# Eight of the twelve transposed chunk pairs turned by the DMA crossbar instead of TensorE

## The chip, the cores and the metric

One core of one Trainium2 chip runs the whole program. The metric is device time in microseconds (us). A run counts as slow when it is over 1.5% above the fastest run of the same kernel.

## The reference, cut to what matters

Two stages. The first is a chunked state-space scan with 4 batches x 8 heads, 768 steps, head width 32 and state width 16. The second is a gated feed-forward over the 3072 x 256 result.

```python
CB = np.einsum('bhin,bhjn->bhij', Cc, Bc)            # C and B of a chunk
M = CB * L                                           # decays and causal mask
y_intra = np.einsum('bhij,bhjd->bhid', M, xc)
y_inter = np.einsum('bhin,bhnd->bhid', Cc, state) * decay_to_i[:, :, :, None]
# ... state update ...
gate = np.maximum(x @ w_gate, 0.0)
val = x @ w_val
return (gate * val @ w_out).astype(np.float32)
```

Both products with C contract over the state dimension, so the kernel needs B and C with the state on the partitions, while they arrive with the tokens on the partitions: each must be turned.

## The kernel before: what the change and the argument touch

The tokens are worked in 12 pairs of 128-token chunks. Pairs 0 to 2 use a wider layout and are not touched. For each later pair GpSimd scales B and C by their decays into a token-major bf16 tile, TensorE turns four 128x128 blocks into PSUM, and ScalarE or VectorE copies them out, C twice, with the heads of the other half zeroed.

```python
def scale_bc(p, eng):
    b, c0 = p // PPB, 2 * (p % PPB)
    s = st[p]
    bs = att.tile([128, 4, 128], BF16, tag="bs", name="bs")
    src = s["bcr"].rearrange("s i j (t q) n -> s (i j) t q n", t=2)
    f = scaleBC[:, b, c0:c0 + 2].rearrange("s c j h -> s (c j) h")
    for t in range(2):
        eng.tensor_tensor(out=bs.rearrange(...)[:, :, t], in0=src[:, :, t], in1=f[...], op=ALU.mult)
    ...
# turn(p):   four nc.tensor.transpose into the PSUM tile "tp"
# tevac(p):  BT <- tp[0] (ScalarE); CT[:, t] <- tp[1] * tmask[:, t] (VectorE, or ScalarE twice)
```

The feed-forward of one 512-token block b is the filler in which the next two pairs, P and Q, are prepared. In the timelines shown below each engine keeps to the program's order (GpSimd: scaling, cast, mask; SyncE: transposes and loads), and SyncE issues nearly all the DMAs from one queue.

```python
for b in range(1, NBLK):
    P, Q, W = 2 * b + 2, 2 * b + 3, 2 * b + 1
    for n in (P + 2, P + 3):
        if n < NPAIR:
            load(n)                                  # 6 DMAs each, on SyncE
    ...
    for f in range(n, NF):
        gv(b, f)                                     # gate and value matmuls
        if b == 1 and at("scale P", 99, 6):
            scale(P, nc.gpsimd, nc.gpsimd)
        if at("scale Q", 9, 6, 4):
            scale(Q, nc.gpsimd, nc.gpsimd)
        if at("scale next P", 11, 11, 9) and P + 2 < NPAIR:
            scale(P + 2, nc.gpsimd, nc.gpsimd)
        if at("turn P", 9, 6, 5):
            turn(P); tevac(P, nc.scalar, nc.vector)
        if at("turn Q", 99, 8, 8):
            turn(Q); tevac(Q, nc.scalar, nc.scalar)
    ...
    inter(P, 0)          # state product, reads CT
    fout(b, 0)
    G(P)                 # B and C product, reads BT and CT
    sums(P); gevac(P)    # gevac: GpSimd's causal mask on part of gs
    ...
    fout(b, 2)
    inter(P, 1)
    Dm(P)                # diagonal product, reads gs
    sums(Q); G(Q)        # (order cut; the details differ by block)
```

## Time and profile before

| what | value |
|---|---|
| time | 127.55 us, median of 3 (126.92 to 127.69) |
| span of the profiled run | 125.4 us |
| TensorE busy | 119.2 us (95%) |
| ScalarE, VectorE, GpSimd busy | 82.0, 88.3, 42.3 us |
| SyncE's DMA queue | 47.9% of 16 engines' span |

TensorE is busy nearly all the time, so a column of busy shares alone says little. The question is where TensorE is ever made to wait. The prediction below shows the lines for that. Two further lines are used later, from the chain of waits (start, length, what): the first half group of block 1 and the last output group. Between these two marks the two kernels differ only by the change.

```profile
32.55 1.99 PE gv L612 x16
...
121.22 1.35 PE o L633 x24
```

The stretch is 121.22 - 32.55 = 88.67 us. What lies ahead of it, the start with its weight loads, is the same code in both kernels apart from four tile clearings on GpSimd.

### The profile page before, as it was taken

What the parts mean: (1) busy time and instruction counts of PE and PEld (TensorE: products, weight loads), DVE (VectorE), ACT (ScalarE), POOL (GpSimd) and SP (SyncE); (2) the same over time, 40 slices, a digit from 0 to 9 for tenths busy, and PEclk for the clock granted to TensorE, in tenths of its full rate; (3) what the DMA queues carried; (4) which work ended last, traced back from release to release, by engine and by line L of the source; (5) the groups of instructions that cost most, each with busy time, mean ns of one, the idle gap of its engine ahead of it and who ended that gap; (6) DMA issues with size and microseconds to landing.
All of it is one profiled execution on the core that took longest, in us unless ns stands there. A gap on an engine that the chain in (4) does not pass through costs nothing.

```text
span 125.4 us, 3648 instructions
## 1 busy us (share of the span) xinstructions
PE 119.2 (95%) x1400; PEld 83.2 (66%) x1400; DVE 88.3 (70%) x196; ACT 82.0 (65%) x185; POOL 42.3 (34%) x86
## 2 busy tenths in 40 slices
PE   6879799899999999999999999999999999999990
PEld 6656585378686578874477865577864577854790
DVE  4795888754799675998673899664989655687510
ACT  0568588835788843787945787935887745876410
POOL 6599863127445016800511801421700033000000
PEclk9999999999999999999999999999999999999999
DMA  3999999987898999196950399920400002200022
GB/s 66 215 172 204 172 216 197 144 106 90 95 105 222 113 116 98 44 200 75 120 70 0 104 167 112 98 40 0 156 16 0 0 0 89 84 0 0 0 89 84
DMA packets 72305, 12.15 MB, mean 97 GB/s; under 512 B 65904, under 2 KB 72288, under 8 KB 72288
## 3 DMA queue, kind: packets, MB, share of 16 engines
q1 hardware_dynamic: 66048, 8.84, 47.9%
q0 software_dynamic: 3184, 2.36, 12.6%
q10 hardware_dynamic: 3056, 0.72, 2.7%
q8 instruction: 11, 0.18, 0.6%
q14 instruction: 6, 0.05, 0.1%
HBM read 11.13 MB, written 3.15 MB: 114 GB/s over the span
## 4 chain that ended last, share of the span: by engine, by line
PE 83%; DMA 9%; ACT 2%; DVE 1%; issue 1%; POOL 1%; DVEq 0%; POOLq 0%
PE o L639 25%; PE gv L612 16%; PE val L597 13%; PE gate L594 13%; DMA wo<-in_moe_w_out_dram 9%; PE w L180 2%; PE y L569 2%; PE g L481 2%; PE tp L321 2%; PE y L558 1%; ACT gs L389 1%; PE o L633 1%; PE g L372 1%; POOL gs L385 1%; PE A_ps L528 1%
## 5 line engine op out<-in xcount | busy, mean ns | idle before, releaser
L601 DVE TENSOR_TENSOR h<-r,val 128x512 bf16<-128x512 bf16 x44 | 29.5, 686 | 8.8 <-ACT r L600 7.2
L639 PE MATMUL o<-wo,h 128*128 128x256 bf16 x276 | 32.8, 273 | 0.5 <-DMA wo<-in_moe_w_out_dram 0.5
L600 ACT ACTIVATE r<-gate 128x512 bf16<-128x512 f32 x44 | 25.9, 600 | 6.0 <-PE gate L594 4.0
L639 PEld LDWEIGHTS <-h 128*128 128x128 bf16 x276 | 25.9, 98 | 5.6 <-issue 1.5
L597 PE MATMUL val<-yT,wv 128*128 128x512 bf16 x88 | 26.2, 379 | 0.0
L594 PE MATMUL gate<-yT,wg 128*128 128x512 bf16 x88 | 26.2, 379 | 0.0
L618 DVE TENSOR_TENSOR h<-r,gv 128x256 bf16<-128x256 bf16 x56 | 22.5, 418 | 2.7 <-ACT r L615 1.8
L615 ACT ACTIVATE r<-gv 128x256 bf16<-128x256 f32 x56 | 21.4, 385 | 2.5 <-PE gv L612 0.4
L612 PE MATMUL gv<-yT,wv 128*128 128x256 bf16 x112 | 21.4, 273 | 0.7 <-DMA wv<-in_moe_w_val_dram 0.7
L612 PE MATMUL gv<-yT,wg 128*128 128x256 bf16 x112 | 21.4, 273 | 0.1
L506 DVE TENSOR_TENSOR gs<-g,maskUT 128x512 bf16<-128x512 f32 x18 | 11.6, 686 | 11.7 <-issue 9.6
L489 POOL TENSOR_SCALAR_AFFINE_SELECT gs<-gs 128x512 bf16<-128x512 bf16 (+1 forms) x18 | 9.0, 523 | 31.3 <-ACT gs L500 31.3
L291 POOL TENSOR_TENSOR bs<-bcr,scaleBC 128x256 bf16<-128x256 f32 x18 | 11.0, 633 | 21.3 <-PE gate L594 6.3
L597 PEld LDWEIGHTS <-wv 128*128 128x128 bf16 x88 | 8.6, 98 | 10.4
L594 PEld LDWEIGHTS <-wg 128*128 128x128 bf16 x88 | 8.2, 98 | 7.0
L612 PEld LDWEIGHTS <-wv 128*128 128x128 bf16 x112 | 10.9, 98 | 2.2 <-DMA wv<-in_moe_w_val_dram 0.9
L612 PEld LDWEIGHTS <-wg 128*128 128x128 bf16 x112 | 10.2, 98 | 2.0 <-issue 0.2
L500 ACT CAST gs<-g 128x512 bf16<-128x512 f32 x9 | 5.3, 589 | 6.7 <-PE g L481 6.7
L582 ACT CAST yT<-y 128x512 bf16<-128x512 f32 x9 | 5.3, 586 | 5.3 <-PE y L569 2.7
L180 PE MATMUL w<-warm 128*128 128x128 bf16 x49 | 5.0, 265 | 1.1 <-DVE tmask L154 1.1
L540 DVE TENSOR_TENSOR Sm<-A_ps,smask 128x256 bf16<-128x256 f32 x15 | 5.7, 415 | 0.0
L180 PEld LDWEIGHTS <-warm 128*128 128x128 bf16 x58 | 4.6, 118 | 1.7 <-DVE tmask L154 1.0
(108 smaller groups left out, 120.6 us busy)
## 6 DMA issues: line engine op xcount, KB each, us to landing
xr<-in_x_dram SPq DMA_DIRECT2D x19, 128.0 KB, 3.8
out_dram<-ob SPq DMA_DIRECT2D x3, 512.0 KB, 3.1
bcr<-in_C_dram SPq DMA_DIRECT2D x19, 64.0 KB, 3.5
bcr<-in_B_dram SPq DMA_DIRECT2D x19, 64.0 KB, 3.7
out_dram<-ob SPq DMA_DIRECT2D x4, 256.0 KB, 2.4
wo<-in_moe_w_out_dram POOLq DMA_DIRECT2D x1, 768.0 KB, 11.0
xr<-in_x_dram SPq DMA_DIRECT2D x2, 256.0 KB, 8.1
wg<-in_moe_w_gate_dram POOLq DMA_DIRECT2D x1, 384.0 KB, 6.2
```

The costliest lines, as they stand in the source:

```text
L180: nc.tensor.matmul(out=w, lhsT=warm, rhs=rhs, start=True, stop=True)
L291: eng.tensor_tensor(out=bs.rearrange("s k (q t n) -> s k t q n", q=4, t=2)[:, :, t], in0=src[:, :, t], in1=f[:, :, 4 * t:4 * t + 4].to_bro ...
L489: nc.gpsimd.affine_select(out=dst, in_=dst, pattern=[[0, n], [1, 128]], compare_op=ALU.is_ge, fill=0.0, base=0, channel_multiplier=-1)
L506: nc.vector.tensor_tensor(out=d[:, q], in0=g[q], in1=m, op=ALU.mult)
L594: nc.tensor.matmul(out=g, lhsT=wg[:, k, fs], rhs=yT[:, k, tk], start=(k == 0), stop=(k == 1))
L597: nc.tensor.matmul(out=v, lhsT=wv[:, k, fs], rhs=yT[:, k, tk], start=(k == 0), stop=(k == 1))
L600: nc.scalar.activation(r, g, AF.Relu)
L601: nc.vector.tensor_tensor(out=fst[b][:, f], in0=r, in1=v, op=ALU.mult)
L612: nc.tensor.matmul(out=gv_[:, j], lhsT=w[:, k, fs], rhs=yT[:, k, tk], start=(k == 0), stop=(k == 1), skip_group_check=True)
L615: nc.scalar.activation(r, gv_[:, 0], AF.Relu)
L618: nc.vector.tensor_tensor(out=fst[b][:, f, u * 256:(u + 1) * 256], in0=r, in1=gv_[:, 1], op=ALU.mult)
L639: nc.tensor.matmul(out=o[:, ts % 2], lhsT=fst[b][:, f, ts * 128:(ts + 1) * 128], rhs=wo[:, f], start=(f == 0), stop=(f == NF - 1), skip_gr ...
```

## The change

The intent is to take 32 transposes off TensorE and the copies behind them off ScalarE and VectorE. The token-major tile is widened to six blocks (B of two chunks, C with the first half of the heads, C with the second half, zeros elsewhere), so that one DMA with transpose (through the crossbar of the title) gives BT and both halves of CT in SBUF. Four such tiles are cleared once; later scalings overwrite only the non-zero parts. In block 1 the loads of pairs 6 and 7 are moved behind the transposes of pairs 4 and 5 respectively.

```diff
+    FIRST = 4
+    NTOK = 4
+    tok = [glob.tile([128, 6, 128], BF16, name="tok%d" % i) for i in range(NTOK)]
     def scale_bc(p, eng):
+        if p >= FIRST:
+            bs = tok[p % NTOK]
+            ...
+            for t in range(2):
+                for j in range(2):
+                    eng.tensor_tensor(
+                        out=dst[:, t, j * (1 + t)], in0=src[:, j, :, t],
+                        in1=f[:, j, :, 4 * t:4 * t + 4].to_broadcast([128, 2, 4, N]),
+                        op=ALU.mult)
+            turned = att.tile([128, 6, 128], BF16, tag="turned", name="turned", bufs=4)
+            nc.sync.dma_start_transpose(out=turned, in_=bs.rearrange("s k c -> s (k c)"))
+            s["B"] = [bs[:, i] for i in range(2)]
+            s["BT"] = turned[:, 0:2]
+            s["CT"] = turned[:, 2:6].rearrange("s (t i) m -> s t i m", t=2)
+            return
@@ before fout(0, 0)
+    for t in tok:
+        nc.gpsimd.memset(t, 0.0)
@@ block loop
-            if n < NPAIR:
+            if n < NPAIR and b > 1:
                 load(n)
@@
             if b == 1 and at("scale P", 99, 6):
                 scale(P, nc.gpsimd, nc.gpsimd)
+                load(P + 2)
             if at("scale Q", 9, 6, 4):
                 scale(Q, nc.gpsimd, nc.gpsimd)
+                if b == 1:
+                    load(P + 3)
@@
-            if at("turn P", 9, 6, 5):
-                turn(P)
-                tevac(P, nc.scalar, nc.vector)
-            if at("turn Q", 99, 8, 8):
-                turn(Q)
-                tevac(Q, nc.scalar, nc.scalar)
```

## The prediction

> **What bounds the kernel now.** I read the engines' busy shares first, then the waits of TensorE, then the chain of waits in order of time, and last the timelines of SyncE and GpSimd around the first turned pairs.
>
> ```profile
> PE 119.2 (95%) x1400; PEld 83.2 (66%) x1400; DVE 88.3 (70%) x196; ACT 82.0 (65%) x185; POOL 42.3 (34%) x86
> ...
> 33.00:122.60 89.60, 89.56 (x943) 62.17 (x941) 64.92 (x131) 61.88 (x136) 22.90 (x42) 1.00 0.48 76
> ```
>
> The first line is the page's busy time; the second is a stretch of the table by windows, from 33.0 to 122.6 us. Over these 89.60 us TensorE is busy 89.56 us at full granted clock, and the list of TensorE's waits for 36 to 118 us is empty. So in the part that the change touches the end is set by the plain sum of TensorE's work: what leaves this stream shortens the kernel one for one, if nothing that it then waits for comes later than now.
>
> ```profile
> 39.17 0.43 PE val L597 x2
> 39.60 0.22 PE tp L321 x4
> 39.83 0.43 PE gate L594 x2
> ...
> 41.55 0.22 PE tp L321 x4
> 41.78 0.43 PE gate L594 x2
> ...
> 48.91 0.28 PE L558 MATMUL y<-CT,Sm 128*128 128x128 bf16 x2
> 49.12 0.41 PE L569 MATMUL y<-gs,xb 128*32 128x128 bf16 x16
> ```
>
> The first lines are the chain (start, length): four transposes of a pair lie between two groups of matmuls and take 0.23 us until the next group starts. The last two are TensorE's timeline at pair 4's diagonal product, which needs the masked tile gs. It starts in the chain at 49.19 us, and no wait is listed.
>
> ```profile
> 46.42 1.20 POOL L291 TENSOR_TENSOR bs<-bcr,scaleBC 128x256 bf16<-128x256 f32 x2 [5.92 <-PE A_ps L528]
> 47.56 0.61 POOL L307 CAST xb<-xr 128x512 bf16<-128x512 f32 x1
> 48.13 1.00 POOL L489 TENSOR_SCALAR_AFFINE_SELECT gs<-gs 128x512 bf16<-128x512 bf16 x2
> ```
>
> This is GpSimd's timeline: scaling pair 6, casting its x, and only then the causal mask of pair 4, finished at 49.13 us, just before TensorE uses it at 49.19. There is no slack here at all: whatever delays pair 6's scaling or cast delays TensorE at pair 4.
>
> ```profile
> 35.82 1.80 SPq L117 DMA_DIRECT2D xr<-in_x_dram  x1
> 37.72 1.04 SPq L679 DMA_DIRECT2D out_dram<-ob  x2
> 38.85 0.44 SPq L116 DMA_DIRECT2D bcr<-in_B_dram  x1
> ...
> 41.63 0.92 SPq L116 DMA_DIRECT2D bcr<-in_C_dram  x1
> 42.59 0.58 SPq L117 DMA_DIRECT2D xr<-in_x_dram  x1
> ...
> 46.87 0.85 SPq L117 DMA_DIRECT2D xr<-in_x_dram  x1
> 51.98 0.38 SPq L657 DMA_DIRECT2D out_dram<-ob  x1
> ```
>
> SyncE's queue issues the loads of pairs 6 and 7 from 38.85 to 47.7 us, with the DMA engines full (share 0.94 to 1.21 from 38 to 48 us, 0.83 to 50, then 0.03 to 52). That is the second thing to watch: the stage has idle DMA time only after 50 us.
>
> **What the Trainium skill says.** "DMA: Bandwidth & Descriptors", section "DMA Transpose (X-bar)": a transpose by DMA must be issued from SyncE or ScalarE, write SBUF and have 2-byte elements; the change does so. The same page, "Latency and other measured facts", gives 261 GB/s as its effective rate with a non-contiguous middle dimension; "Advanced Engine Details and Errata", "X-Bar Transpose (TRN2)", expects 350 to 400 GB/s. No transpose by DMA is in the trace before, so it neither agrees nor disagrees. Third, "Issuing engines are not separate DMA queues" (first page) says that all queues share the same 16 engines; the trace agrees in that loads issued from 38.85 us on take a median 3.6 to 3.7 us to land while the engines are full. Fourth, "TensorE: Matmul & The Clock Gate", "Wait — 56ns, not 53.3ns?", has back-to-back matmuls of N = 128 start 55.6 ns apart; the chain shows 0.22 to 0.23 us for four transposes, 55 to 57 ns each: it agrees, and the 219 ns duration of each is latency.
>
> **The change part by part.**
> Removed from TensorE: 8 pairs x 4 transposes. The chain's eight pieces, each to the start of the next, are 0.23, 0.23, 0.23, 0.22, 0.22, 0.23, 0.22, 0.23 us: 1.81 us, all on the path. That is 1.4% of 127.55 us, and all that can be won.
> Removed from ScalarE: 8 copies of BT at 0.372 us and 8 masked copies of CT (two for each odd pair) at 0.478: 6.8 us. From VectorE: 4 masked copies of CT at 0.685: 2.7 us. Neither engine sets the pace in this stretch (62 and 65 of 90 us busy), so none of the 9.5 us shows in the time.
> Added to GpSimd: four half-size scalings for two, since C's halves go to separate blocks. The two of 128x256 take 1.20 us; pairs of 128x128 in the start took 0.78 to 0.79 us, so four take about 1.57: +0.37 us a pair. For pairs 4 and 5 that is hidden; for pair 6 it lies ahead of pair 4's mask. Four clearings of a 128x768 tile: 128 columns took 0.20 us and 256 took 0.31, so 768 take about 0.75 and four 3.0 us. They fall into GpSimd's 3.85 us of idling from 23.67 to 27.52 us, so cost nothing, with 0.8 us to spare.
> Added to the DMA: eight transposes of 128x768 bf16, 196.6 KB each. At the page's 261 GB/s one occupies the engines 0.75 us (estimate); the rows are cut at 256 bytes and there is the end of each transfer, so I take 1.2 us, with 0.75 to 3 possible.
> Moved: pair 6's loads go behind pair 4's transpose, pair 7's behind pair 5's. Pair 4's tile is scaled at 34.05 + 1.57 = 35.6 us, but SyncE is busy issuing until 38.8; so the transpose goes out at 38.85, behind the 512 KB of output that hold the engines until about 40.2 us. It lands at about 42, and its first reader, the state product, now starts at 44.37 - 0.45 = 43.9: met. Pair 6's loads slip by the same 1.2 us. C was issued at 41.63 and takes a median 3.6 us: 45.2 becomes 46.4; x at 42.59 plus 3.8: 46.4 becomes 47.6. GpSimd: scaling 46.4 to 48.0, cast to 48.6, first mask of pair 4 (0.64 us) to 49.25, second to 49.65. TensorE, now 0.45 us early, arrives at 48.74 and waits 0.5 to 0.9 us. (The old scaling waited for a bs buffer until 46.42; the new tile is free, so that wait falls away and the load takes its place.)
> Pair 5's transpose lands near 48 us; G of pair 5 comes at 49.1 plus the stall: met. Pair 6's goes out after pair 7's loads, about 51 us, and is needed after 62. Pair 7's stands behind pair 9's loads, whose issue ends at 63.0 and whose data end near 64.5; with 1.2 us of its own and the slip still left from earlier it lands about 66 to 67.5, against G of pair 7 at 67.86 - 0.9 + 0.7 = 67.7: just met. Pair 9's lands near 84 against 85.5. Pairs 8, 10 and 11 have 10 us or more.
> Sum: -1.81 + 0.7 for the mask of pair 4 + 0.4 as the expected value for pairs 7 and 9 being now and then late = -0.7 us, 126.9 us.
>
> **The rivals.**
> (a) All transposes hidden: -1.8 us, 125.7 us. For it: pair 6's loads may land well before the medians that I used, since GpSimd in the trace waited for the buffer, not for data, and its cast found x ready. Against it: the mask of pair 4 ended only 0.06 us before its use.
> (b) The transposes hold the DMA engines longer, 2 us each. Then pair 6's loads cost 1.5 us of stall at pair 4, and pair 7's transpose lands at about 69.8 us against 68.5, another 1.3: -1.8 + 2.8 = +1.0, 128.6 us. For it: the engines are full from 38 to 48 us, so every microsecond of transposing moves the loads; the loads themselves are short packets and the skill's rates are for large transfers. At 3 us each this becomes -1.8 + 2.5 + 3 = +3.7, 131 us, and the verdict slower.
> (c) The relief of ScalarE and VectorE gives more than TensorE's 1.8 us. Against it: TensorE has no listed wait in this stretch, so there is nothing to give back. I give it little.
>
> **Range and chances.** From 125.7 (a) to a little above (b), 129.6; the middle is 126.9. Faster by over 2% means below 125.0 us, under the floor of what is removed: 3%, for a gain that I can't see. Slower by over 2% means above 130.1 us, for which a transpose must cost about 2.6 us of engine time or block the queue in a way that I don't foresee: 15%. Within 2%: 82%.
>
> **What would show it.** The chain of the new kernel should have no tp pieces after 31 us, and TensorE should have one or two waits: at the diagonal product of pair 4 on GpSimd's mask (0.5 to 0.9 us near 49 us), and perhaps at G or the state product of an odd pair on the transposing DMA. The landing time of the transposes tells (a) from (b): 2 to 4 us if I am right. GpSimd's scaling of pairs 4 to 11 should show 32 instructions of 128x128 in place of 16 of 128x256, about 1.6 us a pair. I am wrong if TensorE waits for a transpose of pair 4 near 44 us, if the waits sum to over 1.8 us, if the clearings push GpSimd past 27.5 us and delay pair 2's mask, or if the whole gain appears with no wait at all.

## The result, and the profile after

The changed kernel took 125.79 us (median of 4, 125.61 to 126.31) against 127.41 for the kernel before. Ratios in this document are the mean time of one kernel's fast runs over that of the other's of the same rounds, so not quite the ratio of the medians quoted (four_twice is an exception, see there). Here it is 0.9883, 95% interval 0.984 to 0.9927: some 1.5 us, within 2%. All results are correct.

The page's busy line and the long stretch from the table by windows (each engine's busy us, then clock, DMA share, GB/s):

```profile
PE 118.5 (96%) x1368; PEld 82.4 (66%) x1368; DVE 87.3 (70%) x192; ACT 76.8 (62%) x169; POOL 47.2 (38%) x106
...
33.00:120.80 87.80, 87.80 (x911) 60.49 (x910) 63.94 (x127) 56.95 (x120) 25.21 (x58) 1.00 0.57 95
```

TensorE still fills the stretch completely, at full clock, with 32 instructions fewer. ScalarE is 5 us lighter, VectorE 1 us, GpSimd 5 us heavier. The chain at the place where pair 4 was turned, at pair 4's diagonal product, and at the two marks of the stretch:

```profile
32.94 1.99 PE gv L636 x16
...
39.56 0.43 PE val L621 x2
40.00 0.43 PE gate L618 x2
...
49.13 0.34 PE y L593 x16
...
119.83 1.35 PE o L657 x24
```

The tp pieces are gone: a gate group follows the value group at once. The stretch is 119.83 - 32.94 = 86.89 us, 1.78 us shorter than before. The start was 0.39 us longer in this trace.

The turned tile, by its instructions (durations min/median/max in ns), and SyncE's queue line of the page:

```profile
L306 SPq DMA_TRANSPOSE turned<-tok x8: 1219/1231/1363, 38.7 to 88.8; - x8
...
DMA to landing us min/median/max: 2.7/3.2/3.4
```

```profile
q1 hardware_dynamic: 72448, 10.42, 54.7%
```

An issue holds the queue for 1.2 to 1.4 us and the data land 2.7 to 3.4 us after it. The queue took 54.7% of 124.0 us where it was 47.9% of 125.4: 67.8 - 60.1 = 7.8 us, or 0.97 us of packet time on all 16 engines for each transpose. Packet times can overlap (the kernel before has shares up to 1.21), so this is not a time for which the engines were shut to other transfers.

GpSimd and SyncE around pair 4 (timelines; the bracket is the idle time before, and what ended it):

```profile
45.67 1.63 POOL L301 TENSOR_TENSOR tok<-bcr,scaleBC 128x128 bf16<-128x128 f32 x4 [4.92 <-DMA bcr<-in_B_dram]
47.25 0.61 POOL L331 CAST xb<-xr 128x512 bf16<-128x512 f32 x1
47.81 0.99 POOL L513 TENSOR_SCALAR_AFFINE_SELECT gs<-gs 128x512 bf16<-128x512 bf16 x2
```

```profile
38.67 1.36 SPq L306 DMA_TRANSPOSE turned<-tok  x1
40.09 0.57 SPq L116 DMA_DIRECT2D bcr<-in_B_dram  x1
...
42.89 0.58 SPq L116 DMA_DIRECT2D bcr<-in_C_dram  x1
```

The wait for a free bs buffer (5.92 us, ended by the sums of pair 4) has become a wait for pair 6's load, as foreseen. It ended at 45.67 us, so the mask was done at 48.80 and TensorE came at 49.1: 0.3 us to spare, and no wait.

### The profile page after: what moved, and what is told of

It is laid out like the page before. It is cut to its first block, busy times and chain, and to the rows that moved or that the text cites. A ratio compares the mean times of both kernels' runs of the same rounds, so it can differ in the third digit from the quotient of the medians.

```text
span 124.0 us, 3586 instructions
## 1 busy us (share of the span) xinstructions
PE 118.5 (96%) x1368; PEld 82.4 (66%) x1368; DVE 87.3 (70%) x192; ACT 76.8 (62%) x169; POOL 47.2 (38%) x106
## 3 DMA queue, kind: packets, MB, share of 16 engines
q1 hardware_dynamic: 72448, 10.42, 54.7%
## 4 chain that ended last, share of the span: by engine, by line
PE 84%; DMA 7%; POOL 6%; DVE 1%; issue 0%; DVEq 0%; POOLq 0%
PE o L663 25%; PE gv L636 16%; PE val L621 15%; PE gate L618 15%; DMA wv<-in_moe_w_val_dram 7%; PE y L593 2%; PE g L505 2%; PE w L180 2%; POOL wg L189 2%; PE y L582 2%; POOL bs L277 1%; POOL wv L189 1%; PE o L657 1%; PE A_ps L552 1%; POOL xb L328 1%
## 5 line engine op out<-in xcount | busy, mean ns | idle before, releaser
L625 DVE TENSOR_TENSOR h<-r,val 128x512 bf16<-128x512 bf16 x44 | 30.2, 687 | 9.0 <-ACT r L624 7.9
L301 POOL TENSOR_TENSOR tok<-bcr,scaleBC 128x128 bf16<-128x128 f32 x32 | 12.0, 402 | 19.7 <-DMA bcr<-in_B_dram 18.7
L180 PE MATMUL w<-warm 128*128 128x128 bf16 x49 | 6.0, 300 | 1.1 <-DVE tmask L154 1.1
L180 PEld LDWEIGHTS <-warm 128*128 128x128 bf16 x58 | 5.4, 133 | 1.8 <-DVE tmask L154 1.1
```

Source lines behind the costliest of these rows:

```text
L180: nc.tensor.matmul(out=w, lhsT=warm, rhs=rhs, start=True, stop=True)
L301: eng.tensor_tensor(out=dst[:, t, j * (1 + t)], in0=src[:, j, :, t], in1=f[:, j, :, 4 * t:4 * t + 4].to_broadcast([128, 2, 4, N]), op=ALU. ...
L625: nc.vector.tensor_tensor(out=fst[b][:, f], in0=r, in1=v, op=ALU.mult)
```

## The experiments

All outputs are right.

### Is the gain TensorE's stream, and does it repeat?

Four kernels on one chip, five rounds each.

**after_again**: the changed kernel, unedited.

> The changed kernel once more, for a narrower interval. Theory (all eight transposes are hidden, TensorE's stream is 1.8 us shorter): ratio to before 0.986, some 125.7 us, and no wait of TensorE after 33 us. Rival (part of the gain is given back by a wait of about 0.3 to 0.7 us that the first trace did not catch): ratio 0.989 to 0.992.

**pe_turns_kept**: the work on TensorE comes back, result unused.

```diff
+            if at("turn P", 9, 6, 5):
+                spare_turn(P)     # four transposes of a constant tile into "tp"
+            if at("turn Q", 99, 8, 8):
+                spare_turn(Q)
```

> The changed kernel, and TensorE turns a constant tile at the old eight places, result unused (no copies, correct output). Theory (the gain is TensorE's stream alone): 1.8 us come back, ratio to before 0.999 to 1.001, 127.4 us. Rival (the relief of ScalarE and VectorE, 9.5 us of work, carries part of the gain): only part comes back, ratio 0.991 to 0.995.

**copies_kept**: the old copies come back on ScalarE and VectorE, from a constant tile.

```diff
+            if at("turn P", 9, 6, 5):
+                spare_copies(nc.scalar, nc.vector)
+            if at("turn Q", 99, 8, 8):
+                spare_copies(nc.scalar, nc.scalar)
```

> The changed kernel, and ScalarE and VectorE make the old copies of BT and CT at the old eight places from a constant tile, results unused. Theory: nothing changes against the changed kernel, ratio to before 0.986 to 0.988. Rival (relief of the two engines): 0.4 us or more is lost, ratio 0.990 or higher.

**from_pair_6**: pairs 4 and 5 as before, loads of 6 and 7 at their old place.

```diff
-    FIRST = 4
+    FIRST = 6
+            # turn(P)/tevac(P) and turn(Q)/tevac(Q) for pairs under FIRST; load(6), load(7) at the block's top
```

> Pairs 4 and 5 turned by TensorE as before, with the loads of 6 and 7 at their old place; pairs 6 to 11 by the crossbar. Theory: the gain goes by count, 6/8 of 1.8 = 1.35 us, ratio 0.9894, 126.0 us. Rival (the stage of pairs 4 and 5, where the DMA engines are full, costs what it saves): as much as the whole change, 0.986.

| kernel | median us | ratio to before | 95% interval | stretch us | against 88.67 |
|---|---|---|---|---|---|
| after_again | 126.39 | 0.9905 | 0.987 to 0.994 | 87.10 | -1.57 |
| pe_turns_kept | 127.28 | 0.999 | 0.9956 to 1.0023 | 88.68 | +0.01 |
| copies_kept | 126.32 | 0.9906 | 0.9875 to 0.9938 | 86.96 | -1.71 |
| from_pair_6 | 126.57 | 0.9935 | 0.9899 to 0.9971 | 87.70 | -0.97 |

The two marks in the chain of pe_turns_kept:

```profile
32.60 1.99 PE gv L636 x16
...
121.28 1.35 PE o L657 x24
```

With the transposes back on TensorE the stretch is as long as before to 0.01 us, though ScalarE and VectorE stay relieved. With the copies back on those two the ratio equals that of the changed kernel in the same call (0.9906 and 0.9905). Its absolute value lies outside the 0.986 to 0.988 that I had written down, because the changed kernel itself came out slower. So the gain is TensorE's stream alone, and the relief of the two other engines is worth nothing that these runs resolve.

The rule by count gave 1.35 us for six pairs; 0.97 was measured in the trace, 0.8 by the ratio. TensorE has a listed wait there: 0.24 us for VectorE's state tile at the state product of one later pair (88.18 us). The changed kernel's traces, with a TensorE stream that is shorter still, do not have it, so why it came up here is not shown. How the rest is made up was not traced.

The ratio of after_again lies in the rival's range, 0.989 to 0.992. In its trace 0.2 us of the 1.78 was missing, with no wait listed. The traces show the place: from the state product to G of pair 5, TensorE took 0.60 us in the first trace (48.86 to 49.46) and 0.80 in this one (49.08 to 49.88), with the mask done only at 49.55. That is the weak spot that the prediction named.

### Where is the slack, and what sets it?

Four kernels on one chip, three rounds each.

**loads_first**: the change without its reordering.

```diff
-            if n < NPAIR and b > 1:
+            if n < NPAIR:
                 load(n)
-                load(P + 2)       # behind scale(P)
-                if b == 1: load(P + 3)
```

> Changed kernel, but the loads of pairs 6 and 7 are issued at the block's top as before, ahead of the transposes of pairs 4 and 5. Theory (the queue is served in order, and 9 us of loads stand in it): pair 4's transpose is issued at about 47.7 us and lands 3.2 us later, 50.9, against its first use near 44.1: one wait of 6 to 7 us at the state product of pair 4, ratio to before about 1.04. Rival (order doesn't matter, a transpose of 0.8 to 1.2 us finds its way): ratio 0.99.

**four_twice**: pair 4's tile is turned twice.

```diff
+            if p == FIRST:
+                spare = att.tile([128, 6, 128], BF16, tag="spare", name="spare", bufs=1)
+                nc.sync.dma_start_transpose(out=spare, in_=bs.rearrange("s k c -> s (k c)"))
             nc.sync.dma_start_transpose(out=turned, in_=bs.rearrange("s k c -> s (k c)"))
```

> Changed kernel with pair 4's tile turned twice (first into a spare tile). Everything behind it in the queue, pair 6's loads first, slips by 1.25 us. Theory (pair 6's loads hold GpSimd, which stands between TensorE and pair 4's mask, with 0.3 us to spare at most): TensorE waits 0.7 to 1.2 us near 49 us at pair 4's diagonal product, +0.9 us against the changed kernel, ratio to before about 0.996. Rival (the loads have over 1 us of slack): no wait, ratio 0.989.

**four_twice_mask_first**: the same, with GpSimd's work on pair 6 moved behind pair 4's mask.

```diff
-            if at("scale next P", 11, 11, 9) and P + 2 < NPAIR:
+            if b > 1 and at("scale next P", 11, 11, 9) and P + 2 < NPAIR:
                 scale(P + 2, nc.gpsimd, nc.gpsimd)
@@ behind gevac(P) and states(P) of block 1
+                scale(P + 2, nc.gpsimd, nc.gpsimd)
```

> As four_twice, but GpSimd scales and casts pair 6 after pair 4's mask. Theory: the wait at pair 4's diagonal product is gone though the loads slip as much, ratio 0.988 to 0.990. Rival (the wait is one of the DMA or of the transposes of pairs 5 and 7 themselves): it stays, ratio 0.995 or more.

**twice**: every tile turned twice.

```diff
+            for _ in range(1):
+                spare = att.tile([128, 6, 128], BF16, tag="spare", name="spare", bufs=4)
+                nc.sync.dma_start_transpose(out=spare, in_=bs.rearrange("s k c -> s (k c)"))
             nc.sync.dma_start_transpose(out=turned, in_=bs.rearrange("s k c -> s (k c)"))
```

> Changed kernel with every tile turned twice. Theory: +0.9 us at pair 4's mask, up to 0.6 at pair 5's G, 1 to 2 at pair 7's G (its transpose lands at 66.3 against 67.4 in the changed kernel, and slips by 2.5): 2 to 3.5 us in all, 128 to 129.5 us, ratio 1.005 to 1.018. Rival (the DMA has room; only pair 4's stage is tight): +0.9 us, ratio 0.996.

| kernel | median us | ratio to before | 95% interval |
|---|---|---|---|
| loads_first | 135.66 | 1.0595 | 1.0509 to 1.0681 |
| four_twice | 128.97 (126.67 to 132.05) | 1.0082 (see below) | 1.0003 to 1.0161 |
| four_twice_mask_first | 129.29 | 1.0095 | 1.0011 to 1.0179 |
| twice | 131.53 | 1.0283 | 1.0205 to 1.0361 |

**loads_first.** TensorE's timeline has one wait, and the page's row of the granted clock shows what came after it:

```profile
51.09 0.40 PE L582 MATMUL y<-turned,Sm 128*128 128x128 bf16 x2 [7.12 <-DMA turned<-tok]
...
PEclk9999999999999955599999999999999999999999
```

The wait is 7.1 us where 6 to 7 were expected: the transpose was issued at 47.73 us behind the loads and landed at 51.04. The reordering of the loads is therefore worth more than the whole gain. The ratio was underestimated, 1.04 against 1.06. The clock row shows what the expectation had left out: for three slices of 3.3 us TensorE ran at about half its clock, part of it while waiting and part of it afterwards.

**twice.** The theory put the loss against the changed kernel at 2 to 3.5 us, a ratio of 1.005 to 1.018. The ratio is 1.0283: 3.6 us over the kernel before and, with the changed kernel's ratios of 0.9883 to 0.9933, 4.5 to 5.1 over the changed kernel. The trace is that of the fastest run (129.88 us, the others 131.47 to 131.74). TensorE's waits, and the table by windows for the time around them (TensorE's busy us stands second, the clock third from the end):

```profile
49.70 0.65 PE L596 MATMUL y<-gs,xb 128*32 128x128 bf16 x16 [0.80 <-POOL gs L516]
...
51.67 0.40 PE L508 MATMUL g<-turned 32*128 32x256 bf16 x8 [1.26 <-DMA turned<-tok]
```

```profile
48.00:50.00 2.00, 1.20 (x19) 0.92 (x17) 0.27 (x1) 0.10 (x1) 2.00 (x5) 1.00 1.31 76
50.00:52.00 2.00, 0.71 (x24) 0.35 (x23) 0.00 (x0) 0.59 (x1) 0.01 (x1) 1.00 1.06 111
52.00:54.00 2.00, 2.00 (x17) 1.57 (x14) 1.78 (x4) 0.86 (x2) 1.00 (x2) 0.69 1.17 108
54.00:56.00 2.00, 2.00 (x13) 1.39 (x10) 0.60 (x2) 1.19 (x3) 0.98 (x3) 0.50 1.35 155
```

The waits stand at the expected places: 0.8 us at pair 4's mask (0.9 expected), 1.3 at G of pair 5 (up to 0.6) and 0.2 at G of pair 7 (1 to 2). After them the clock falls to half. From the clock column of these windows and the next (0.95) that costs 2 x (0.31 + 0.50 + 0.05) = 1.7 us, so it lasts some 3.4 us (estimates). The stretch was 91.25 us, 4.36 longer than in the first changed trace: about 2.3 us of listed waits and 1.7 of clock; the rest, some 0.4 us, was not traced.

**four_twice and four_twice_mask_first.** The first one's profile fell in a run that counts as slow (132.05 us). That trace shows TensorE 3.1 us at pair 4's mask, but I take no size from it. The expected +0.9 us against the changed kernel cannot be judged from its fast runs either: there are two, 126.67 and 128.25. They average 127.46 us against 127.58 for the kernel before, 0.999, so the recorded 1.0082 can't be theirs alone, and I don't use it. The second was meant to remove the wait by moving GpSimd's work, and by that test the theory failed. The mask no longer held TensorE, but another wait stood next to it:

```profile
51.67 0.40 PE L508 MATMUL g<-turned 32*128 32x256 bf16 x8 [1.68 <-DMA turned<-tok]
...
70.21 0.40 PE L508 MATMUL g<-turned 32*128 32x256 bf16 x8 [0.64 <-DMA turned<-tok]
```

Pair 5's transpose landed 5.1 us after its issue (46.55 to 51.63), not 3.2. With 3.2 us it would have landed at 49.75, before TensorE came at 49.99 (51.67 - 1.68). So this wait comes from the late landing and not from the slip of the queue alone. In twice it is the same: 46.84 + 3.2 = 50.04, and TensorE came at 50.41. Pair 7's transpose took its usual 3.2 us but was issued late, at 66.93 us instead of 63.08. The stretch was 89.35 us, 2.46 longer than in the first changed trace, with 2.3 us of it in these two waits. The rival was half right: what held TensorE was transposes, but how much the slip alone would cost is not shown.

One thing stands beside both late landings. The rate of all transfers in twice, from 38 to 54 us in slices of 0.4 us:

```profile
GB/s 107 234 346 330 335 224 209 139 148 212 132 40 97 88 102 109 149 155 116 98 93 148 169 220 211 117 232 22 1 9 35 201 139 108 71 115 164 142 90 29
```

From 48.8 to 50.4 us it falls to 22, 1, 9 and 35 GB/s, while transposes stand unfinished. The trace's list of DMA packets has one of 16 KB, of the queue that the page calls instruction (q8), from 48.64 to 49.60 us; in four_twice_mask_first it runs from 48.40 to 49.65, with 1 to 10 GB/s from 49.2 to 50.4. In the three traces of the changed kernel this packet starts at 48.67 to 48.90, after pair 5's transpose has landed (47.82 to 48.70). That it holds the transposes up is likely but was not tested.

### With both edges moved

Four kernels on one chip, five rounds each. **before_again** is the kernel before against itself and **after_third** the changed kernel, both unedited.

> The kernel before against itself, as a check of the scatter and for a second trace of its start. Ratio 1.000 plus or minus 0.003. If the start up to the first half group of block 1 is again at 32.5 us, and the changed kernel's again at 32.9 or later, the start costs the changed kernel 0.4 us; if it moves by as much here, it is scatter of the weights' arrival.

> The changed kernel a third time beside the other three of this call. Theory: from the first half group of block 1 to the last output group 1.6 to 1.8 us shorter than before (88.67 us there), ratio 0.986 to 0.990.

**mask_first**: the edit of four_twice_mask_first without the second turning of pair 4.

> Changed kernel, but GpSimd scales and casts pair 6 after pair 4's mask. Theory: pair 4's mask no longer can hold TensorE, worth 0 to 0.2 us: the same stretch is 1.75 to 1.8 us shorter than before, ratio within 0.002 of the changed kernel. Rival (something else held TensorE in the second trace): the stretch is 0.2 us longer again.

**both_first**: mask_first, and the transposes of pairs 4 and 5 both ahead of the loads of 6 and 7.

```diff
             if b == 1 and at("scale P", 99, 6):
                 scale(P, nc.gpsimd, nc.gpsimd)
-                load(P + 2)
             if at("scale Q", 9, 6, 4):
                 scale(Q, nc.gpsimd, nc.gpsimd)
                 if b == 1:
+                    load(P + 2)
                     load(P + 3)
```

> Transposes of pairs 4 and 5 both ahead of the loads of 6 and 7, and pair 4's mask ahead of pair 6's scaling. Theory: all waits in the stage get 1 us of slack or more, but there is nothing left to win beyond the 1.8 us: ratio within 0.002 of the changed kernel, no wait of TensorE after 33 us. Rival (the faster runs of the changed kernel are those without a late landing): 0.2 to 0.4 us faster than the changed kernel in the median.

| kernel | runs, us | ratio to before | 95% interval | stretch us |
|---|---|---|---|---|
| before_again | 126.56 to 127.82, median 127.18 | 0.9967 | 0.9925 to 1.0008 | 88.68 |
| after_third | 126.24 126.25 127.01 128.01, slow: 128.99 129.14 | 0.9933 | 0.9873 to 0.9993 | 87.38 |
| mask_first | 124.99 to 126.00, median 125.71 | 0.9836 | 0.9797 to 0.9875 | 87.37 |
| both_first | 125.25 to 125.77, slow: 127.24 | 0.9822 | 0.9783 to 0.9862 | 87.03 |

A difference of 0.3% between equal kernels is scatter, as before_again shows. The expectation for after_third was missed: 0.9933 for 0.986 to 0.990, and a stretch 1.29 us shorter for 1.6 to 1.8. The changed kernel was the least steady of the four. Its third trace shows the weak spot once more, on GpSimd and on TensorE:

```profile
48.04 0.61 POOL L331 CAST xb<-xr 128x512 bf16<-128x512 f32 x1
48.60 1.00 POOL L513 TENSOR_SCALAR_AFFINE_SELECT gs<-gs 128x512 bf16<-128x512 bf16 x2
```

```profile
48.84 0.28 PE L582 MATMUL y<-turned,Sm 128*128 128x128 bf16 x2
49.29 0.65 PE L593 MATMUL y<-gs,xb 128*32 128x128 bf16 x16 [0.18 <-POOL gs L513]
...
49.94 0.40 PE L505 MATMUL g<-turned 32*128 32x256 bf16 x8
```

The mask ended at 49.60 us, and from the state product to G took 1.10 us against 0.60 in the first trace. So half a microsecond was lost although only 0.18 is listed as a wait; the rest lies inside the slower group of diagonal products. mask_first takes that dependence away:

```profile
46.11 1.00 POOL L513 TENSOR_SCALAR_AFFINE_SELECT gs<-gs 128x512 bf16<-128x512 bf16 x2 [5.71 <-ACT gs L524]
47.07 1.49 POOL L301 TENSOR_TENSOR tok<-bcr,scaleBC 128x128 bf16<-128x128 f32 x4
```

```profile
67.07 0.40 PE L505 MATMUL g<-turned 32*128 32x256 bf16 x8 [0.41 <-DMA turned<-tok]
```

The mask is done at 47.1 us, 1.3 us before TensorE comes for it (48.37). In its trace the next edge shows: G of pair 7 waited 0.41 us for its transpose, the place that the prediction called "just met". So its stretch is 1.30 us shorter than before, not the 1.75 that was expected. In both_first's trace TensorE has no listed wait in the stretch, as expected, and it is 1.64 us shorter.

Both reordered kernels beat both kernels. Over fast runs mask_first averages 125.63 us and both_first 125.46, against 126.88 for the changed kernel in the same call. Their ratios lie under the floor that the prediction sets (0.9855), but the runs that they are divided by were 0.3% longer than those of before_again: against its 127.18 they gain 1.5 and 1.7 us, not more than the 1.81 taken off TensorE. I had expected no measurable difference from the changed kernel, so that theory failed; the rival, that the changed kernel loses something in part of its runs, had 0.2 to 0.4 us for it, and the difference is at least three times that. The traces show 0 to 0.5 us of it at pair 4's mask. They don't show the whole 1.2 us. The traces of mask_first and both_first also have a shorter start, 32.24 and 32.32 us up to the first mark against 32.92 to 33.15 in the three traces of the changed kernel, with the same code there. The kernel before moved by as much between its own two traces (32.55 and 31.97), so I take the start for scatter. What share of the 1.2 us is start and what share lies at the edges of runs without a trace stays open.

## Why the prediction was right, and where its sizes were off

The time, 125.79 us, lies in the range 125.7 to 129.6 at its lower end, and the verdict was the likely one. The middle, 126.9, was 1.1 us too high. The mechanism held: TensorE's stream sets the time, and what is taken off it comes back one for one less what is then waited for. Two terms for those waits were too large. And one of the prediction's own signs of being wrong, "the whole gain appears with no wait at all", is what the first trace shows.

- **Removed from TensorE, 1.81 us.** Right: the stretch shrank by 1.78 us, and grew back to +0.01 when the transposes were put back unused. (The last of the eight pieces reads 0.22 us, not 0.23, so the sum is 1.80.)
- **The relief of ScalarE and VectorE shows nothing (rival c).** Right: putting their copies back changed the ratio by 0.0001. Their busy time fell by 5.2 and 1.0 us (82.0 to 76.8, 88.3 to 87.3), less than the 6.8 and 2.7 that I counted out. A part of that is the view, which counts overlapping time once (ten masked copies of 0.479 us have 4.2 us of busy time); the rest was not looked into, as it shows in no time.
- **GpSimd's clearings and scalings.** The four clearings took 2.8 us for an estimated 3.0, from 23.19 to 25.96 us, inside the idle time. Four scalings took 1.48 to 1.63 us for an estimated 1.57.
- **A transpose takes 1.2 us of the engines and lands after some 3 us.** Near: 0.97 us and 2.7 to 3.4. Rival (b) with 2 us and a loss of 1.0 us against before has its nearest test in `twice`: by the queue's share 2.5 us a tile ((62.5% of 128.2 - 60.1) / 8, with the packets that stood still), and 3.6 us lost. It named pair 4's mask, took pair 5's transpose as met where 1.3 us were lost, put 1.3 us at pair 7 where 0.2 was lost, and did not know of the clock.
- **Pair 4's mask, +0.7 us.** This is the term that was mis-sized. I put the start of pair 6's scaling at 46.4 us, the end of the mask at 49.65 and TensorE's arrival at 48.74. The three traces have the scaling at 45.67, 46.29 and 46.40, and the end of the mask at 48.80, 49.55 and 49.60. In the first trace C was issued at 42.89 us, 1.26 later than before, and landed after 3.2 us where I had used the median of 3.6; and I had let the whole scaling wait for C, while B's part starts without it (46.29 in after_again, C's at 46.93). In the other two traces GpSimd was nearly as late as I said. There the loss was smaller because TensorE came later, at 49.3 and 49.1 us: the start of all three traces was 0.4 to 0.6 us longer than in the kernel before. The loss was 0, 0.2 and 0.5 us. That it was 0 in the first trace, and the time at the lower end of the range, was luck.
- **Pairs 7 and 9 now and then late, +0.4 us.** Not seen in the three traces of the changed kernel. Pair 7's G did wait 0.4 us in mask_first and 0.2 in twice; pair 9 never did.
- **The third point from the Trainium skill**, that all queues share the same 16 engines: the trace before does not show it where the prediction looks. From 38 to 50 us all of its packets but one are those of SyncE's queue.

So the first result was nearly rival (a), with everything hidden; the changed kernel came out at 0.9883, 0.9905 and 0.9933, all between the floor (125.7 / 127.55 = 0.9855) and the predicted middle (126.9 / 127.55 = 0.995).

## What to carry to other kernels

When the bounding engine has no waits, the gain from taking work off it is the sum of the removed pieces of its chain, and nothing from engines beside it; put the removed work back unused to prove it. A replacement that goes through a shared in-order queue must be judged by what it delays behind it: here the next loads, through them GpSimd, and through GpSimd's program order a mask that TensorE needed. Look for the places where an engine's order puts work for later ahead of work for now, since moving one such piece gave 124.99 to 126.00 us where the changed kernel took 126.24 to 129.14, though the traces account for only a part of that.

## What the Trainium skill lacked or had wrong

- "DMA: Bandwidth & Descriptors", "Latency and other measured facts": 261 GB/s for a transpose, and 350 to 400 in "Advanced Engine Details and Errata", "X-Bar Transpose (TRN2)". Here 196.6 KB took 0.97 us of packet time on the 16 engines (worked out from the queue's shares above), some 203 GB/s (estimate), beside loads in short packets.
- The same two places give no time for the issue of such a transpose on this chip; a table about trn3 on the first page has cycle counts of earlier chips for other shapes only. In the first trace it held SyncE's queue for 1.22 to 1.36 us, where a load's issue between 38 and 50 us took 0.57 to 0.58 at its shortest. The load of C behind it was issued 1.26 us later than in the kernel before (42.89 for 41.63) and landed 0.9 us later.
- "TensorE: Matmul & The Clock Gate", "What's actually happening", has the array fall back to half clock after an idle window of about 3.4 us. In `twice` waits of 0.80 and 1.26 us, with TensorE busy 1.91 us of the 4 us around them, were followed by a clock of 0.69 and then 0.50, without any idle time of 3.4 us. A single wait of 1.68 us in four_twice_mask_first was not: the clock of that run was 1.0. The half clock itself agrees with the page. No run here fixes the limit.
- No page says that a transpose can stand still beside an instruction fetch. Landings that mostly took 2.7 to 3.4 us took 5.1 in four_twice_mask_first and 4.8 in twice, both ending at 51.6 us, with a 16 KB packet of the instruction queue in their midst and almost no data moving for over a microsecond. The cause was not tested.
